# Re-timing a projection, a load and some sums in an attention + FFN kernel whose instructions stay the same

## The chip, the cores and the metric

The kernel runs on one core of a Trainium2 chip. The metric is device time in microseconds (us). TensorE (PE) does the matmuls, VectorE (DVE) and ScalarE (ACT) read their results from PSUM, GpSimd (POOL) issues the loads that also convert f32 to bf16, and SyncE (SP) issues the other DMAs.

## The reference

Linformer attention (8 batches, 8 heads, 1024 tokens, head size 64, keys and values projected to 64 rows), then a feed-forward layer with a squared relu (512 to 2048 to 512):

```python
k_proj = einsum('ks,bhsd->bhkd', E, k);  v_proj = einsum('ks,bhsd->bhkd', F, v)
attn   = softmax(q @ k_proj^T / sqrt(64))          # per batch and head
x      = (attn @ v_proj) as (8*1024, 512)
out    = square(max(x @ w_in, 0)) @ w_out
```

## The kernel before

After a start-up stretch of about 109 us, a steady loop runs on PE: every *step* issues four 128x256 matmuls of the first FFN product (line 652) and, in most steps, four of the second (line 572). Both products use a seven-product (Strassen-like) scheme, so PSUM results are copied from bank to bank, and sums of inputs are formed on DVE. A batch takes 56 steps. Attention for the coming batches is put in between by a plan of steps; PE's order is exactly the order of the code, while the other engines' orders are chosen by a scheduler from the dependencies.

The parts that matter:

```python
def project(self):                       # k and v of a batch, into one PSUM bank
    ps = att_psum()[:, 0]                # (in the loop there is one such buffer)
    for i in range(NI):
        ...matmul(ps[LO, :], lhsT=ET, rhs=self.K...)       # k: partitions 0-63
        ...matmul(ps[HI, :], lhsT=FT, rhs=self.V...)       # v: partitions 64-127
    for g in range(2):
        self.keep_k(ps[LO, ...], g)      # casts "kp", two on DVE for each g
    self.keep_v(ps[HI, :])

def keep_v(self, ps_v):
    nc.scalar.copy(self.vp[HI], view)    # cast "vp" on ACT
    nc.vector.tensor_copy(self.vp[LO], view)

# second FFN product, "second_spread": the seed
yield from product(1, first, True)
nc.scalar.copy(chain, first)             # the seed copy, on ACT
yield
yield
yield from product(2, first, two=True)   # 8 matmuls in a row, may start only after the seed copy
...
# first FFN product, one group = 7 steps: p1, p5, p4 (of the group before), p6, p2, p3, p7
# p1 -> ACT copy; p5, p6 -> ACT copy "u"; p2, p4 -> ACT relu "h"; p3, p7 -> DVE relu-sum "h"
...
for b in range(1, B - 1):                # the plan, t = first step of the batch
    ...
    on(t + 3, b + 1, "sums_spread", 2)   # ends in 8 small DMAs, the "spread copies" rs<-inv
    on(t + 7, b + 1, "values", 0); ... on(t + 23, b + 1, "values", 3)      # DVE needs rs
    for c in range(2):
        at(t + 24 + 9 * c, ... chunk[b + 1, c].sum_x())    # four sums on DVE
    ...
        on(t + 3, b + 3, "load_q")
    on(t + 30, b + 2, "project")
    on(t + 32, b + 2, "transpose_k_dma") # kT<-kp, a transposing DMA, needed at t + 44
        on(t + 34, b + 3, "load_kv")
    on(t + 44, b + 2, "scores", 0)
```

A load goes out when its buffer is free, not at its step: the step sets only its place in POOL's queue.

The softmax here doesn't subtract the row's maximum and nothing guards it: scores larger than these inputs give would overflow.

Of the kernel before, what the change touches and what calls it, by code (L numbers as in the profile page):

```python
# [12 lines left out]
AF = mybir.ActivationFunctionType  # L13
# [6 lines left out]
def kernel(  # L20
# [11 lines left out]
    nc = tc.nc  # L32
# [15 lines left out]
    SCALE = 1.0 / float(D) ** 0.5  # L48
# [26 lines left out]
    def att_psum():  # L75
        turn["att"] += 1
        return pair_psum(turn["att"] % turn["pairs"])

    def bank(shape=(P, 512), dtype=F32, n=None):
        if n is None:  # L80
            turn["bank"] += 1
            n = turn["bank"]
        return psum.tile(list(shape), dtype, tag=f"bank{n % 4}", name="ps_bank")

    def tokens(src, b, h=slice(None), i=slice(None)):
        return src[b].rearrange("h (p i) d -> p h i d", i=NI)[:, h, i, :]

    def load(t, src):
        return nc.gpsimd.dma_start(t, src)

    def load_batch(name, src, b):
        t = qkv_pool.tile([P, H, NI, D], BF16, name=name)
        load(t[:], tokens(src, b))
        return t


# [30 lines left out]
    for j, (lo, hi) in enumerate(W_IN_PIECES):  # L127
        t = wpool.tile([P, NCB, (hi - lo) * P], BF16, name=f"w_in_{lo}")
# [6 lines left out]
    for j in range(WP):  # L135
        if j == WP - 1:
            load(Q0[:, :, 4:8, :], tokens(q, 0, i=slice(4, 8)))
        t = wpool.tile([P, fn, DM], BF16, name=f"w_out_{j}")
# [83 lines left out]
    class Attention:  # L222
# [10 lines left out]
            self.qT = qt_pool.tile([P, H, NT, P], BF16, name="qT")  # L233
            self.e, self.rs, self.ps_x = {}, {}, {}

        def load_kv(self):
            self.K, self.V = load_batch("K_sb", k, self.b), load_batch("V_sb", v, self.b)

        def load_q(self):
            self.Q = load_batch("Q_sb", q, self.b)  # L240


        def keep_k(self, ps_k, g, second=None):
# [96 lines left out]

        def exponentials(self, ps):
            e = soft_pool.tile([P, 2, TCH], BF16, name="expT", tag="expT", bufs=4)
            nc.scalar.activation(e[:], ps[:], AF.Exp, scale=SCALE)  # L343
            return e

        def inverse(self, ps):
# [49 lines left out]
        def values(self, pr, spare=False):  # L396

            e, rs = self.e.pop(pr), self.rs.pop(pr)
            if spare:
                ps_x = [bank(), bank()]  # L400
            else:
                ps = att_psum()
                ps_x = [ps[:, par] for par in range(2)]
            for o, par, a, r in VALUE_QUADS:
                nc.tensor.matmul(  # L405
                    ps_x[par][o], lhsT=self.vp[r, 2 * pr + a, :], rhs=e[r, par], start=True, stop=True
                )
            for par in range(2):
                nc.vector.tensor_tensor(  # L409
                    out=self.xT[:, pr, :, par], in0=ps_x[par].rearrange("p (c t) -> p c t", c=2),  # L410
                    in1=rs[:, par].rearrange("p (c t) -> p c t", c=2), op=ALU.mult,
                )
# [295 lines left out]
    with tc.manual_schedule(engines={PE}):  # L708
# [30 lines left out]
        def at(step, fn, *args, **kwargs):  # L739
            plan.setdefault(step, []).append(lambda: fn(*args, **kwargs))  # L740
# [13 lines left out]
        atts = {0: att}  # L754
        chunk = {(0, c): Chunk(att, c) for c in range(2)}
# [104 lines left out]
        def on(step, b, name, *args):  # L860
            at(step, lambda: getattr(atts[b], name)(*args))

        for b in range(1, B - 1):
            t = 56 * (b - 1)
            if b > 1:
                on(t + 1, b + 1, "scores", 3)
            on(t + 3, b + 1, "sums_spread", 2)
            on(t + 7, b + 1, "values", 0)
            on(t + 10, b + 1, "values", 1)
            on(t + 20, b + 1, "values", 2)  # L870
            on(t + 23, b + 1, "values", 3)
            for c in range(2):
                at(t + 24 + 9 * c, lambda b=b, c=c: chunk[b + 1, c].sum_x())
            if b + 2 < B:
                on(t + 2, b + 2, "transpose_q_dma")
                if b + 3 < B:
                    at(t + 2, begin, b + 3)
                    on(t + 3, b + 3, "load_q")
                on(t + 30, b + 2, "project")
                on(t + 32, b + 2, "transpose_k_dma")  # L880
                if b + 3 < B:
                    on(t + 34, b + 3, "load_kv")
                on(t + 44, b + 2, "scores", 0)
                on(t + 47, b + 2, "scores", 1)
                on(t + 50, b + 2, "sums_spread", 0)
                on(t + 53, b + 2, "scores", 2)
# [34 lines left out]
```

## Time and profile before

482.11 us, median of 3 runs (481.99 to 482.15). From the page: the span, PE's busy time, and the chain of work that ended last by engine.

```profile
span 479.9 us, 10022 instructions
PE 469.9 (98%) x4106; PEld 352.0 (73%) x4106; DVE 350.1 (73%) x613; ACT 286.8 (60%) x466; POOL 32.5 (7%) x45
PE 86%; DVE 8%; ACT 4%; issue 1%; DMA 1%; DVEq 0%; ACTq 0%
```

PE is the limit. How much is still to be had is not told by "98% busy": a pipelined matmul is drawn longer than the time it takes its turn. The Trainium skill ("Trainium Kernel Development and Optimization", Best Practices) says to judge by MFU (the share of the peak matmul rate that is used) and by the busy share of the weight loads, 73% here, and not by that of the matmuls. For small stalls I used another measure, the distance from one start to the next: a 128x256 matmul starts 0.109 us after the one before it, so four take 0.437 us. What exceeds that is a stall, or the change to a differently tiled matmul.

The list of waits, PE alone (columns: us in total, times, longest us):

```profile
PE ps_second L572 <- ACT ps_second L588: 1.3, 5, 0.3
```

The same stall in the timelines, once per batch. PE (start, duration, and in brackets the idle time and what ended it):

```profile
196.59 0.60 PE L572 MATMUL ps_second<-w_out,h 128*128 128x256 bf16 x4
197.03 0.60 PE L652 MATMUL ps_bank<-xT,w_in_sum 128*128 128x256 bf16 x4
197.47 0.60 PE L652 MATMUL ps_bank<-x_sum,w_in_sum 128*128 128x256 bf16 x4
198.33 1.03 PE L572 MATMUL ps_second<-w_out,h 128*128 128x256 bf16 x8 [0.26 <-ACT ps_second L588]
```

The first three groups start 0.44 us apart; product 2 starts 0.86 us after the group before it, so 0.42 us is lost. The bracket says 0.26 because it counts from the drawn end of the matmul. And ACT in the same place:

```profile
195.04 0.60 ACT L662 ACTIVATE h<-ps_bank 128x512 bf16<-128x512 f32 x1 [2.08 <-PE ps_bank L652]
195.97 0.59 ACT L544 COPY u<-ps_bank 128x512 f32<-128x512 f32 x1 [0.33 <-PE ps_bank L652]
196.58 0.58 ACT L251 CAST vp<-ps_att 64x512 bf16<-64x512 f32 x1
197.19 0.60 ACT L662 ACTIVATE h<-ps_bank 128x512 bf16<-128x512 f32 x1
197.69 0.59 ACT L588 COPY ps_second<-ps_second 128x512 f32<-128x512 f32 x1
```

Before a seed that has no projection near it, ACT's timeline has no vp:

```profile
417.10 0.59 ACT L544 COPY u<-ps_bank 128x512 f32<-128x512 f32 x1 [0.33 <-PE ps_bank L652]
417.92 0.60 ACT L662 ACTIVATE h<-ps_bank 128x512 bf16<-128x512 f32 x1 [0.23 <-PE ps_bank L652]
418.41 0.59 ACT L588 COPY ps_second<-ps_second 128x512 f32<-128x512 f32 x1
```

There relu and copy wait for PE, not PE for them. The cast in front of the relu is what makes the seed late.

### The profile page before, as it was taken

To read this page: it belongs to the slowest core of one execution; us is meant where nothing else is said; L and a number is where in the kernel's file an instruction comes from. 1 tells how busy PE (TensorE), PEld (TensorE's weight loads), DVE (VectorE), ACT (ScalarE), POOL (GpSimd) and SP (SyncE) were. 2 spreads that over 40 slices of the span, in tenths; PEclk is the share of its full clock that TensorE was granted. 3 is DMA by queue.
4 is the path that set the end of the run, shared out by engine and by line. 5 is a ranking of instruction groups with operands and counts; after the bars stand their busy time and mean duration, and the time that the engine had idled before them with its cause. 6 is when DMAs were issued, how large, how long until landed. Compare 5 with 4: busy or idle time off the path is not lost.

```text
span 479.9 us, 10022 instructions
## 1 busy us (share of the span) xinstructions
PE 469.9 (98%) x4106; PEld 352.0 (73%) x4106; DVE 350.1 (73%) x613; ACT 286.8 (60%) x466; POOL 32.5 (7%) x45
## 2 busy tenths in 40 slices
PE   8999999999999999999999999999999999999996
PEld 3444445537878788787878778787887778888885
DVE  2456897956996679767897579966797678967671
ACT  2464467397547774578546785477745775565641
POOL 7410010200010000100010000100000000000000
PEclk9999999999999999999999999999999999999999
DMA  9999998999949496767939499495811054101012
GB/s 177 204 206 205 229 165 142 180 225 190 197 83 171 124 200 163 124 130 180 201 105 185 90 221 175 96 160 139 205 54 55 23 133 111 67 23 67 24 66 89
DMA packets 80046, 66.98 MB, mean 140 GB/s; under 512 B 30720, under 2 KB 76032, under 8 KB 80000
## 3 DMA queue, kind: packets, MB, share of 16 engines
q0 software_dynamic: 30640, 29.23, 39.3%
q1 hardware_dynamic: 49216, 36.97, 29.2%
q8 instruction: 32, 0.52, 0.4%
q10 hardware_dynamic: 144, 0.13, 0.1%
q14 instruction: 14, 0.11, 0.1%
HBM read 59.24 MB, written 16.78 MB: 158 GB/s over the span
## 4 chain that ended last, share of the span: by engine, by line
PE 86%; DVE 8%; ACT 4%; issue 1%; DMA 1%; DVEq 0%; ACTq 0%
PE ps_bank L652 34%; PE ps_second L572 33%; PE ps_bank L489 6%; PE ps_att L329 2%; PE ps_att L258 2%; PE ps_second L549 2%; PE ps_att L405 2%; DVE rs L373 1%; DVE w_in_sum L150 1%; DVE w_out_sum L150 1%; DVE xT L434 1%; DVE h L150 1%; PE ps_bank L216 1%; ACT h L485 1%; PE ps_att L382 1%
## 5 line engine op out<-in xcount | busy, mean ns | idle before, releaser
L150 DVE TENSOR_TENSOR h<-h 128x1024 bf16<-128x1024 bf16 (+1 forms) x182 | 108.0, 616 | 39.8 <-ACT h L662 26.0
L652 PE MATMUL ps_bank<-x_sum,w_in_sum 128*128 128x256 bf16 x624 | 93.9, 273 | 0.0
L652 PEld LDWEIGHTS <-w_in_sum 128*128 128x128 bf16 x832 | 78.7, 98 | 16.2 <-issue 7.5
L572 PEld LDWEIGHTS <-h 128*128 128x128 bf16 x832 | 81.3, 98 | 11.8 <-issue 2.2
L544 ACT COPY u<-ps_bank 128x512 f32<-128x512 f32 x107 | 63.2, 591 | 26.0 <-PE ps_bank L652 23.1
L662 ACT ACTIVATE h<-ps_bank 128x512 bf16<-128x512 f32 x104 | 62.9, 605 | 26.3 <-PE ps_bank L652 25.9
L666 DVE CUSTOM_DVE_ANT_0 h<-ps_bank,u 128x512 bf16<-128x512 f32 x104 | 68.9, 685 | 12.5 <-PE ps_bank L652 11.9
L677 ACT COPY ps_bank<-ps_bank 128x512 f32<-128x512 f32 x52 | 29.7, 570 | 68.9 <-PE ps_bank L652 68.9
L652 PEld LDWEIGHTS <-w_in 128*128 128x128 bf16 x624 | 58.8, 98 | 13.9 <-issue 7.2
L572 PEld LDWEIGHTS <-s 128*128 128x128 bf16 x624 | 61.1, 98 | 7.1
L652 PE MATMUL ps_bank<-xT,w_in 128*128 128x256 bf16 x416 | 62.5, 273 | 0.0
L572 PE MATMUL ps_second<-w_out_sum,s 128*128 128x256 bf16 x416 | 62.4, 273 | 0.0
L572 PE MATMUL ps_second<-w_out_sum,h 128*128 128x256 bf16 x416 | 62.2, 273 | 0.0
L572 PE MATMUL ps_second<-w_out,h 128*128 128x256 bf16 x416 | 60.1, 272 | 1.3 <-ACT ps_second L588 1.3
L409 DVE TENSOR_TENSOR xT<-ps_att,rs 128x512 bf16<-128x512 f32 x56 | 36.0, 684 | 15.9 <-PE ps_att L405 15.9
L489 PE MATMUL ps_bank<-xT,w_in 128*128 128x512 bf16 x192 | 45.3, 379 | 1.8 <-DVE xT L434 1.0
L485 ACT ACTIVATE h<-ps_bank 128x512 bf16<-128x512 f32 x48 | 28.1, 605 | 16.1 <-PE ps_bank L489 15.9
L150 DVE TENSOR_TENSOR o_sb<-ps_second,u 128x512 f32<-128x512 f32 x27 | 18.5, 685 | 25.9 <-PE ps_second L572 20.7
L489 PEld LDWEIGHTS <-w_in 128*128 128x128 bf16 x192 | 17.7, 98 | 24.6 <-issue 6.2
L343 ACT ACTIVATE expT<-ps_att 128x1024 bf16<-128x1024 f32 x32 | 32.9, 1036 | 2.9 <-PE ps_att L329 2.5
L652 PE MATMUL ps_bank<-x_sum,w_in 128*128 128x256 bf16 x208 | 31.4, 273 | 0.0
L652 PE MATMUL ps_bank<-xT,w_in_sum 128*128 128x256 bf16 x208 | 31.3, 273 | 0.0
(104 smaller groups left out, 477.7 us busy)
## 6 DMA issues: line engine op xcount, KB each, us to landing
out_dram<-o_sb SPq DMA_DIRECT2D x63, 256.0 KB, 2.4
rs<-inv SPq DMA_DIRECT2D x96, 128.0 KB, 2.9
K_sb<-in_k_dram POOLq DMA_DIRECT2D x7, 1024.0 KB, 9.7
V_sb<-in_v_dram POOLq DMA_DIRECT2D x7, 1024.0 KB, 15.7
Q_sb<-in_q_dram POOLq DMA_DIRECT2D x7, 1024.0 KB, 12.7
w_out<-in_moe_w_out_dram POOLq DMA_DIRECT2D x4, 512.0 KB, 17.5
w_in<-in_moe_w_in_dram POOLq DMA_DIRECT2D x3, 512.0 KB, 14.6
k_f<-in_k_dram SPq DMA_DIRECT2D x1, 512.0 KB, 4.6
```

Source lines behind the costliest of these rows:

```text
L150: return nc.vector.tensor_tensor(out=o, in0=x, in1=y, op=op)
L258: nc.tensor.matmul(ps[LO, :], lhsT=ET[:, i, :], rhs=self.K[:, :, i, :], start=f, stop=l)
L343: nc.scalar.activation(e[:], ps[:], AF.Exp, scale=SCALE)
L409: nc.vector.tensor_tensor(out=self.xT[:, pr, :, par], in0=ps_x[par].rearrange("p (c t) -> p c t", c=2), in1=rs[:, par].rearrange("p (c t) ...
L485: nc.scalar.activation(h, ps.rearrange("p (a t) -> p a t", a=2), AF.Relu)
L489: nc.tensor.matmul(ps[:], lhsT=w_in_blk(cb, fb), rhs=self.xT[:, cb, self.c].rearrange("p a t -> p (a t)"), start=(cb == 0), stop=(cb == NC ...
L544: nc.scalar.copy(u[:], ps)
L572: nc.tensor.matmul(ps[:, i * HM:(i + 1) * HM], lhsT=self.h_form(n, fb)[:, i * P:(i + 1) * P], rhs=w_out_form(n, fb), start=fresh and i == ...
L652: nc.tensor.matmul(ps[:, j * HC:(j + 1) * HC], lhsT=w_in_form(n, cb, 2 * self.g + j), rhs=self.chunk.x_form(n, cb), start=fresh and j == 0 ...
L662: nc.scalar.activation(self.out(kh, a), ps[:], AF.Relu)
L666: nc.vector._custom_dve(TENSOR_ADD_SAT, out=self.out(kh, a), in0=ps[:], in1=more[:], s0=3.0e38, s1=0.0)
L677: nc.scalar.copy(self.chain[:], self.first[:])
```

## The change

Its intent: project k and v two steps sooner, so that the casts are out of the way when the seed is due; hold q's load back from the spread copies; form the second chunk's x sums later, so that DVE is free at the seed.

```diff
-    def load_batch(name, src, b):
+    def load_batch(name, src, b, behind=None):
         t = qkv_pool.tile([P, H, NI, D], BF16, name=name)
-        load(t[:], tokens(src, b))
+        dma = load(t[:], tokens(src, b))
+        if behind:
+            tc.add_manual_dep(dma.ins, behind().ins.name, ..., reason="load behind")
         return t
...
-                nc.vector.tensor_tensor(
+                self.done = nc.vector.tensor_tensor(          # in values()
...
-                at(t + 24 + 9 * c, lambda b=b, c=c: chunk[b + 1, c].sum_x())
+                at(t + 24 + 12 * c, lambda b=b, c=c: chunk[b + 1, c].sum_x())
...
-                    on(t + 3, b + 3, "load_q")
-                on(t + 30, b + 2, "project")
-                on(t + 32, b + 2, "transpose_k_dma")
+                    on(t + 11, b + 3, "load_q", lambda b=b: atts[b + 1].done)
+                on(t + 28, b + 2, "project")
+                on(t + 30, b + 2, "transpose_k_dma")
                 if b + 3 < B:
-                    on(t + 34, b + 3, "load_kv")
+                    on(t + 32, b + 3, "load_kv")
```

No instruction is added or removed. At step t + 11 the last `done` is that of the second pair of heads (`values` at t + 10).

## The prediction

> **What bounds the kernel.** TensorE: the page gives PE busy 469.9 of 479.9 us, and the chain of waits is 86% PE. The Trainium skill ("Trainium Kernel Development and Optimization", Best Practices) says matmul busy time is no measure of headroom; weight loads are busy 73% here. So I read the distance between matmul starts. In the timeline of the steady loop (109 to 411 us, period 55.77 us) the 128x256 products start every 0.109 us. Besides about 0.4 us for each switch to attention's smaller tiles, one stall stands out: five times product 2 of the second stream (8 matmuls, L572) waits for ACT's seed copy (L588). At 198.33 it starts 0.42 us later than the cadence wants; the other four lose as much. Total: 2.1 us. (The list of waits shows 1.3 us, since it counts from the end of the pipelined matmul.)
>
> **Why the seed is late.** ACT's timeline: u at 195.97, v's cast vp (L251, 0.58 us) at 196.58, relu at 197.19, seed at 197.69 to 198.28. Where no projection is near (169.07, 418.41) the order is u, relu, seed; the seed starts 0.37 us after product 1's last matmul starts, against 0.77 us at 197.69, and product 2 loses only 0.01 to 0.03 us. So the cast costs 0.40 us.
>
> **What the change does.** No instruction is added or removed; order moves.
> 1. Projection about 1.75 us earlier. The built order on ACT becomes relu(p4), vp, u(p6), relu(p2), seed: vp goes where ACT idles (2.08 us before 195.04). Estimate from the durations: vp 195.55, u 196.1, relu 196.8, seed 197.3. Worth 5 x 0.40 = 2.0 us, all on PE's path.
> 2. Second chunk's x sums later: two of the four sums (0.42 us each on DVE) come after the relu-sums of p3 and p7 instead of before. Before, p3's relu-sum ends at 199.88 and PE needs the bank at 200.07; with PE 0.4 us earlier this would have become the next wait. Estimate for the new order: it ends near 199.2, needed at 199.65. Earns nothing alone, protects the gain.
> 3. q's load behind DVE's values: it already waited for q's transposing DMA (issued at 174.55); now 1 to 2 us later, used some 45 us later. Worth 0. k and v's loads start 1.75 us earlier. The transposing DMA of k takes 9 us beside them (196.07 to 205.07; 2.3 us at 363.35, where no load runs), needed at 207.15: slack 2 us, should stay over 1.
>
> The first 138 us and the tail keep their order.
>
> **Prediction.** 482.1 - 2.0 = 480.1 us, 0.4% faster; range 479.6 to 481.3. Chances: faster by over 2% 0.01, within 2% 0.97, slower 0.02.
>
> **What would show it.** PE L572's wait for the seed falls from 1.3 us to nearly nothing; the period falls to about 55.37; the seed starts 0.37 us after product 1's last matmul everywhere; matmul counts stay. Step 1 is wrong if the wait stays, step 2 if PE waits for DVE's relu-sum (L666 before) at p5, step 3 if scores wait for kT or DVE's values for rs.
>
> **What would make it wrong.** ACT's and DVE's casts of the projection holding each other up, so that ACT is late again (gain 0 to 1 us); the projection waiting for the attention bank's last values; kT late; DVE's backlog at 186 to 200 us, busy almost without a gap, moving a relu-sum onto PE's path.

## The result, and the profile after

481.11 us, median of 4 runs (479.92 to 481.53), against 482.05 us before. The ratio is 0.998, 95% interval 0.9959 to 1.0002. By time alone this is "the same"; the trace is finer. Line numbers are 5 higher than before. From the page:

```profile
span 479.1 us, 10022 instructions
PE 469.1 (98%) x4096; PEld 351.9 (73%) x4106; DVE 349.2 (73%) x613; ACT 286.2 (60%) x466; POOL 33.3 (7%) x45
PE 86%; DVE 8%; ACT 3%; issue 1%; DMA 1%; DVEq 0%; ACTq 0%
```

(Ten matmul records are missing from this trace; the weight loads, 4106, are all there.) The wait of PE for the seed copy is gone from the list of waits, but not from the cadence. PE's timeline:

```profile
196.73 0.60 PE L577 MATMUL ps_second<-w_out,h 128*128 128x256 bf16 x4
197.16 0.60 PE L657 MATMUL ps_bank<-xT,w_in_sum 128*128 128x256 bf16 x4
197.60 0.60 PE L657 MATMUL ps_bank<-x_sum,w_in_sum 128*128 128x256 bf16 x4
198.22 1.03 PE L577 MATMUL ps_second<-w_out,h 128*128 128x256 bf16 x8
```

Product 2 starts 0.62 us after the group before it, so 0.18 us is still lost where it was 0.42. The period of the loop (seed to seed, 141.91 to 197.69 before and 142.03 to 197.56 after) went from 55.77 to 55.53 us: 0.24 us in each of five batches, 1.2 us in all, not 2.0. The span shows 0.8 because this run's start-up happened to be 0.37 us longer (first seed at 113.67 instead of 113.30): from the first seed to the end of the span it is 366.6 us before and 365.4 after, which is the 1.2. ACT tells why 0.18 us stayed:

```profile
195.18 0.60 ACT L667 ACTIVATE h<-ps_bank 128x512 bf16<-128x512 f32 x1
195.98 0.58 ACT L256 CAST vp<-ps_att 64x512 bf16<-64x512 f32 x1 [0.21 <-DVE kp L252]
196.59 0.58 ACT L549 COPY u<-ps_bank 128x512 f32<-128x512 f32 x1
197.07 0.60 ACT L667 ACTIVATE h<-ps_bank 128x512 bf16<-128x512 f32 x1
197.56 0.61 ACT L593 COPY ps_second<-ps_second 128x512 f32<-128x512 f32 x1
```

The cast vp did move in front of u, as foretold, but ACT then stood idle until DVE's last cast of kp (L252) had ended. DVE's timeline:

```profile
192.64 0.69 DVE L155 TENSOR_TENSOR s<-h 128x1024 bf16<-128x1024 bf16 x1
193.25 0.41 DVE L251 CAST kp<-ps_att 64x256 bf16<-64x256 f32 x1
193.58 0.67 DVE L155 TENSOR_TENSOR s<-s,h 128x1024 bf16<-128x1024 bf16 x1
194.18 0.67 DVE L155 TENSOR_TENSOR h<-h 128x1024 bf16<-128x1024 bf16 x1
194.78 0.41 DVE L252 CAST kp<-ps_att 64x256 bf16<-64x256 f32 x1
195.20 0.42 DVE L251 CAST kp<-ps_att 64x256 bf16<-64x256 f32 x1
195.54 0.41 DVE L252 CAST kp<-ps_att 64x256 bf16<-64x256 f32 x1
```

The projection was done on PE near 192.8, but the scheduler put a sum (`s<-s,h`) and a squaring (`h<-h`), 0.67 us each, between the casts of kp, so the last of them ends at 195.95, and vp at 195.98 follows it at once. In the built program that cast waits on DVE's semaphore alone, not on PE's: two engines' reads of one PSUM bank (the only tile that the two casts share) are put in order. The Trainium skill ("PSUM — Partial Sum Buffer", PSUM bank collisions raise a hardware error) says that reads by ScalarE and VectorE of the same bank and the same 32-partition quadrant collide and that software has to keep them apart, while different quadrants run clean. Here kp is read from partitions 0 to 63 and vp from 64 to 127. No run here tried the two reads at once.

### The profile page after: what moved, and what is told of

Read it like the earlier page. It is cut to its first block, busy times and chain, and to the rows that moved or that the text cites. A ratio compares the mean times of both kernels' runs of the same rounds, so it can differ in the third digit from the quotient of the medians.

```text
span 479.1 us, 10022 instructions
## 1 busy us (share of the span) xinstructions
PE 469.1 (98%) x4096; PEld 351.9 (73%) x4106; DVE 349.2 (73%) x613; ACT 286.2 (60%) x466; POOL 33.3 (7%) x45
## 4 chain that ended last, share of the span: by engine, by line
PE 86%; DVE 8%; ACT 3%; issue 1%; DMA 1%; DVEq 0%; ACTq 0%
PE ps_bank L657 35%; PE ps_second L577 33%; PE ps_bank L494 6%; PE ps_att L334 2%; PE ps_att L263 2%; PE ps_second L554 2%; PE ps_att L410 2%; DVE rs L378 1%; DVE w_in_sum L155 1%; DVE w_out_sum L155 1%; DVE xT L439 1%; DVE h L155 1%; PE ps_bank L221 1%; DMA e_f<-in_E_dram 1%; ACT h L490 1%
```

## The experiments

My theory after the result, A: the wait of ACT's vp for DVE's kp is what left the 0.18 us. Rival B: ACT's u and relu are late on their own. A second question was which part of the change earned the 0.24 us. "Period" is always seed to seed in the trace, a figure that repeated within 0.01 us in undisturbed batches; whole times of one kernel on one chip scatter by 2 to 3 us.

### 1. v's casts first

```diff
-            for g in range(2):
-                self.keep_k(ps[LO, g * C // 2:(g + 1) * C // 2], g)
-            self.keep_v(ps[HI, :])
+            self.keep_v(ps[HI, :])
+            for g in range(2):
+                self.keep_k(ps[LO, g * C // 2:(g + 1) * C // 2], g)
```

> The changed kernel with one more edit: in the projection, v's casts stand before k's casts, so ACT's cast of vp no longer waits for DVE's last cast of kp. Theory A (the 0.18 us that product 2 still loses per batch comes from that wait): ACT's vp starts about 192.8 us, in its idle time; the seed starts 0.37 us after product 1's last matmul; product 2 loses under 0.05 us; the period falls from 55.53 to about 55.37, total gain against the kernel before about 2.0 us. Rival B (seed late because ACT's u and relu are late on their own): vp moves, but product 2 still loses 0.18 us and the period stays 55.53. A side effect to watch under both: DVE casts kp later, so k's transposing DMA starts about 0.5 us later, and its slack ahead of the scores (0.8 to 1.1 us now) falls to 0 to 0.5 us; if it is used up, scores wait for kT.

Measured: period 55.37 in all batches, product 2 loses 0.03 us, the seed starts 0.37 us after product 1's last matmul. A holds, B falls. The slack of k's transposing DMA stayed at 0.7 to 0.8 us, although it was issued later; see experiment 2. The whole time, however, was 480.85 us (before on that chip 481.01; ratio 0.9981, interval 0.9963 to 0.9999), hardly better than the change itself. The list of waits for PE shows what was given back, a wait in the start-up, which uses the same function:

```profile
PE ps_bank L293 <- DVE kp L252: 1.1, 1, 1.1
```

There PE waits for kp at once, and v's cast now delays kp: 1.1 us instead of 0.2.

### 2. ... and the loads of k and v behind k's transposing DMA

To experiment 1 this adds

```diff
-            nc.sync.dma_start_transpose(                       # transpose_k_dma
+            self.done = nc.sync.dma_start_transpose(
-                    on(t + 32, b + 3, "load_kv")
+                    on(t + 32, b + 3, "load_kv", lambda b=b: atts[b + 2].done)
```

> As vfirst, and the loads of the next k and v wait until k's transposing DMA has landed, so that the two do not run at once. If k's transposing DMA takes 9 to 10 us only because the loads run beside it: it lands in 2 to 3 us, slack ahead of the scores over 7 us; period 55.37 or lower if vfirst shows scores waiting for kT, else the same as vfirst. Rival (the transposing DMA is slow by itself when ACT and DVE are busy): still 9 to 10 us to landing.

Measured: period 55.37; 480.16 us, ratio 0.9972 (0.9955 to 0.9990). The view of the tile kT gives the time from issue to landing, first for the changed kernel, then for this one:

```profile
DMA to landing us min/median/max: 2.3/10.1/10.3
```

```profile
DMA to landing us min/median/max: 2.3/2.3/2.4
```

So the 10 us are the company of the loads. The Trainium skill ("DMA: Bandwidth & Descriptors", Issuing engines are not separate DMA queues) says that DMAs of all issuing engines share 16 DMA engines and interleave; these traces agree and give the price for a small transfer beside a large load, a factor of about 4. The slack ahead of the scores went from 0.7 to 7.6 us, which bought no time: it had not been negative.

### 3. v's casts first in the kernel before, projection unmoved

> The kernel before, with only the order of the casts turned (v's before k's); the projection stays where it was. Theory A says that the position of vp's cast on ACT is all that matters for the seed: vp moves ahead of relu(p4), about 194.6 to 195.2, the seed is on time (0.37 us after product 1's last matmul) without moving the projection. But DVE then casts kp 1.3 us later and squares h after that (about 197.3 to 198.0), which product 2 needs at 197.9: I expect a loss of 0 to 0.3 us per batch there, and k's transposing DMA about 1.3 us later, its slack 2.0 falls to about 0.3. Period 55.4 to 55.7. Rival (moving the projection is what matters, not the cast's place): period stays 55.77.

Measured: the seed was on time (0.37 us, loss 0.03), so for the seed the cast's place is what matters, and not the projection's. But the kernel was slower: 484.17 us, ratio 1.0049 (1.0030 to 1.0068), period 56.10, well over the 55.7 that I had allowed. PE's timeline shows two new losses, one inside product 2 (1.16 us where 1.03 is normal) and one at p5, where the bracket says 0.39 us and the distance of starts 0.55:

```profile
199.39 1.16 PE L572 MATMUL ps_second<-w_out,h 128*128 128x256 bf16 x8
201.82 0.60 PE L652 MATMUL ps_bank<-x_sum,w_in_sum 128*128 128x256 bf16 x4 [0.39 <-DVE h L666]
```

I had expected the first and overlooked the second: the casts of kp, now late, push p3's relu-sum (L666), whose bank p5 needs. The projection's earlier place serves DVE, not ACT; experiment 7 shows that moving the sums relieves DVE too.

### 4. The projection's move alone

> The kernel before with the projection (and with it k's transposing DMA and the loads of k and v) two steps earlier, and nothing else of the change. My theory: all of the gain is here, period 55.53, as with the whole change; p3's relu-sum on DVE ends near 199.5, PE needs the bank near 199.9, so no wait yet. Rival (the x sums are needed at this speed already): PE waits for DVE's relu-sum at p5 and the period is above 55.6.

Measured: period 55.53, product 2 loses 0.18 us; 480.14 us, ratio 0.9973 (0.9953 to 0.9993). All of the change's gain per batch is in this part. (Its lower time is a luckier start: first seed at 112.24; from there to the end it is 365.4 us, as with the whole change.)

### 5. The sums' move alone, and the load of q alone

Each is one line (or, for q, the load and its dependency) of the diff applied to the kernel before; one run each.

> The kernel before with the second chunk's x sums twelve steps on and nothing else. Theory: worth nothing alone, since product 2's wait for the seed (0.42 us) leaves the order on ACT as it was: period 55.77. Rival (DVE's backlog delays the casts and through them the seed): the sums' move frees DVE and the loss falls below 0.4 us.

> The kernel before with only the load of q behind the values. Theory: period 55.77, q's load starts 0 to 3 us later in each batch, nobody waits for it. Rival (the load of q slows the spread copies or the transposing DMA, so that moving it pays): period below 55.7, or the spread copies landing sooner.

Measured: period 55.77 in both, product 2 loses 0.42 to 0.43 us in both. Alone, neither is worth anything. Single times, 482.32 and 481.91 us beside 482.77, are within the scatter.

### 6. v's casts first in the loop only

```diff
-        def project(self):
+        def project(self, v_first=False):
...
+            if v_first:
+                self.keep_v(ps[HI, :])
             for g in range(2):
                 self.keep_k(ps[LO, g * C // 2:(g + 1) * C // 2], g)
-            self.keep_v(ps[HI, :])
+            if not v_first:
+                self.keep_v(ps[HI, :])
...
-                on(t + 28, b + 2, "project")
+                on(t + 28, b + 2, "project", True)
```

> The changed kernel with v's casts first, but only for the projections inside the steady loop; before the loop the casts keep their old order. In vfirst the loop took 55.37 us per batch, but the stretch before the loop lost about 1.0 us: there, transposes of kp on PE waited 1.11 us for DVE's cast instead of 0.21 us. Theory: both are had now, period 55.37 and that wait back at 0.21 us; the fixed part before the loop as in the kernel before within its run-to-run scatter; about 2.0 us under the kernel before and about 0.8 us under the changed kernel. Rival (the loss before the loop is part of the scatter of the start): no better than vfirst.

> vfirst_loop again, unedited, beside vfirst_loop_dma on one chip. Expected: period 55.37 in most batches, a ratio to the kernel before of about 0.9955 as at first (0.9952, interval 0.9930 to 0.9973); the difference to vfirst_loop_dma under 0.3 us if the late spread copies are as rare as they look.

> The changed kernel again, unedited, beside the others on one chip, since its first timing had an interval of plus or minus 0.2%. If its gain is 5 times 0.24 us per batch as its trace says, the ratio of the means is near 0.9975, and any further difference is scatter of the start (the first seed copy fell between 112.2 and 114.4 us in six profiled runs whose code there is nearly the same). If the period is not 55.53 again, the reading of the trace was wrong.

Measured, first call, one chip: this version 480.14 us, ratio 0.9952 (0.9930 to 0.9973); the changed kernel again 481.28 us, ratio 0.9981 (0.9961 to 1.0000); the kernel before 482.05 us. In the second, this version gave 480.23 against 481.77 us, ratio 0.9967 (0.9950 to 0.9984). The wait in the start-up is back at 0.2 us, the period, from the second seed on, is 55.37 in all but one batch. Its ACT timeline shows that ACT's idle time before vp is now ended by PE and not by DVE, and PE's that product 2 starts 0.46 us after the group before it:

```profile
192.31 0.58 ACT L256 CAST vp<-ps_att 64x512 bf16<-64x512 f32 x1 [3.46 <-PE ps_att L264]
195.50 0.59 ACT L552 COPY u<-ps_bank 128x512 f32<-128x512 f32 x1 [0.33 <-PE ps_bank L660]
196.31 0.60 ACT L670 ACTIVATE h<-ps_bank 128x512 bf16<-128x512 f32 x1 [0.23 <-PE ps_bank L660]
196.81 0.59 ACT L596 COPY ps_second<-ps_second 128x512 f32<-128x512 f32 x1
```

```profile
196.99 0.60 PE L660 MATMUL ps_bank<-x_sum,w_in_sum 128*128 128x256 bf16 x4
197.45 1.03 PE L580 MATMUL ps_second<-w_out,h 128*128 128x256 bf16 x8
```

By the period this version beats both kernels: five batches times 0.40 us against the kernel before, which is the sum that I had predicted for the change. In the trace of the second the whole of it arrives: 364.6 us from the first seed to the end against 366.6 before. In that of the first it is 365.2, since besides the one late batch PE lost 0.42 us at 114.8, waiting for ACT's inv (L394), which had waited for spread copies. By time it beats the kernel before in both. Its lead over the changed kernel in the first, 1.3 us between the means of six runs each, is barely clear of the scatter (plus or minus 1.3, worked out from the twelve times).

### 7. The sums put back, once the seed is on time; and the sums moved in experiment 3

> vfirst_loop with the second chunk's x sums back at their old step. It tests what the prediction said of them: that they earn nothing alone but become the next wait once PE is 0.4 us earlier. In vfirst p3's relu-sum on DVE ends at 199.96 and PE needs its bank at 200.29; the old step puts one more sum (0.34 us from start to start) ahead of it, so it ends near 200.30. Expected: PE waits at p5 for DVE's relu-sum, 0.05 to 0.15 us per batch, period 55.42 to 55.52. Rival (the sums never mattered): period 55.37.

> The kernel before with v's casts first in the loop and the x sums twelve steps on, the projection unmoved. In vfirst_before (without the sums moved) the seed was on time but PE waited 0.39 us at p5 for DVE's relu-sum of p3, and product 2 came 0.13 us later in its middle: period 56.10. Here the relu-sum stands ahead of three sums and should end near 0.6 us before PE needs it: the wait at p5 goes, only the loss in product 2 (h squared after the casts of kp) stays. Period 55.45 to 55.6. Rival (DVE is late for other work than the sums): the wait at p5 stays above 0.2 us.

Measured: 55.50 in both. In the first, 0.13 us per batch is lost, all of it ahead of p5 and the p4 after it (0.065 us each), because p3's relu-sum comes one x sum later on DVE, and p7's two. In the second, PE no longer waits at p5 (0.39 us by the bracket before), and only product 2's 0.12 us is left. So the sums' move is worth 0.13 us per batch at the pace of experiment 6, 0.6 us in experiment 3 (56.10 to 55.50), and nothing at the pace of the kernel before.

### 8. A late batch in two traces

In the repeat of the changed kernel one batch of four took 56.17 instead of 55.53 us, and in the first trace of experiment 6 one took 55.47. Both times DVE had waited near 242 us for spread copies. The repeat, first DVE, then ACT ten us later:

```profile
242.57 1.29 DVE L414 TENSOR_TENSOR xT<-ps_att,rs 128x512 bf16<-128x512 f32 x2 [1.22 <-DMA rs<-inv]
```

```profile
251.97 0.58 ACT L256 CAST vp<-ps_att 64x512 bf16<-64x512 f32 x1 [0.86 <-DVE kp L252]
```

DVE, which is busy there almost without a gap, carried the 1.2 us along, kp came late, vp waited 0.86 us for it, and product 2 came late. In experiment 6, where vp does not wait for kp, a wait of 0.94 us cost only 0.10 us. Why were the copies late? (The longest that any of the traces shows after the start-up took 9.7 us.) The next version moves the load of q to step t + 24, behind the values of the *last* pair, and has the loads of k and v wait as in experiment 2.

```diff
-                    on(t + 11, b + 3, "load_q", lambda b=b: atts[b + 1].done)
+                    on(t + 24, b + 3, "load_q", lambda b=b: atts[b + 1].done)
```

> vfirst_loop with two loads moved: q's load waits for the values of the last pair instead of the second pair (so all spread copies of the inverse sums have landed), and the loads of k and v wait until k's transposing DMA has landed. Question: why did DVE wait 1.22 us and 0.94 us once each (in the traces of after_again and vfirst_loop, near 242 us) for the last spread copies? Theory: q's load still starts while the last copies are in flight[...]; landing is within 1 us of the need in every batch with a load. Expected: the last copy of each group lands within 3 us of its issue, 5 us or more before it is needed; k's transposing DMA lands in 2 to 6 us; no wait of DVE for rs; period 55.37 in all batches; time as vfirst_loop or up to 0.3 us less. Rival (the copies are slow by themselves behind the stores on the same queue): still 10 us or more.

Measured: the view of the tile rs between 109 and 300 us, where batches have a load of q, first experiment 6, then this one:

```profile
DMA to landing us min/median/max: 2.2/2.6/9.4
```

```profile
DMA to landing us min/median/max: 2.2/2.5/4.1
```

Each group's last copy now lands 2.3 to 2.4 us after its issue and more than 5 us before the values that need it; in all the other kernels it landed 0.1 to 1.8 us before them wherever a load of q was under way. Experiment 2 held back the loads of k and v alone, and its copies still took up to 8.2 us; so it is the load of q, and the rival, the stores on the same queue, which are there in both, falls. k's transposing DMA lands in 2.3 to 3.9 us. No wait for rs, and 55.37 or 55.38 in all batches. The time, 479.67 us, ratio 0.9958 (0.9938 to 0.9978), cannot be told from that of experiment 6 on the same chip (480.23 us, 0.9967): this is insurance, not speed.

### Summary

| version | period, us | product 2 loses, us | ratio to before |
|---|---|---|---|
| before | 55.77 | 0.42 | 1 |
| the change | 55.53 | 0.18 | 0.9980, again 0.9981 |
| its projection alone | 55.53 | 0.18 | 0.9973 |
| its sums alone; its load of q alone | 55.77 | 0.42 | one run each |
| change, v's casts first everywhere | 55.37 | 0.03 | 0.9981 |
| ... with the loads of k and v held back | 55.37 | 0.03 | 0.9972 |
| before, v's casts first everywhere | 56.10 | 0.03 | 1.0049 |
| change, v's casts first in the loop | 55.37 | 0.03 | 0.9952, again 0.9967 |
| ... with the loads of q, k and v held back | 55.37 | 0.03 | 0.9958 |
| change, v's casts first in the loop, its sums put back | 55.50 | 0.03 | one run |
| before, v's casts first in the loop, sums moved | 55.50 | 0.03 | one run |

## Why the prediction was right or wrong, point by point

- **The time**: 480.1 was predicted with 479.6 to 481.3; 481.11 was measured. Right, but by the width of the range: the middle was 1 us too low. There is luck in it too: the first seed alone falls anywhere within 2 us from run to run, the range was 1.7 us wide, and one of the four runs (481.53) lay outside it. By time alone the result can't be told from no change; the period tells it.
- **What bounds the kernel, and why the seed is late**: right. The cast vp costs the seed 0.40 us; experiments 1 and 6 got back exactly that by moving this one cast. A slip of wording: the "0.4 us for each switch to attention's smaller tiles" contains the attention matmuls' own time and is not all switching cost.
- **Step 1, "5 x 0.40 = 2.0 us"**: right mechanism, wrong size. The term that failed is "vp 195.55, u 196.1, ... seed 197.3". Measured: vp 195.98, u 196.59, seed 197.56 (this trace runs about 0.13 us later there). I had vp follow relu(p4) at once, and had not seen that the built program lets it wait for DVE's last cast of kp, which stood behind a sum and a squaring of h. The gain was 0.24 us a batch, 1.2 us in all. I named this danger among what would make it wrong ("casts of the projection holding each other up") and still put the full sum in the middle.
- **Step 2, the sums "earn nothing alone, protect the gain"**: right. Alone 0; at the full pace 0.13 us a batch. At the pace that the change really reached they were not yet needed (experiment 4).
- **Step 3, the loads**: worth 0 alone, right. "Slack 2 us, should stay over 1" was wrong in three of four batches with loads: 0.77, 0.79, 1.09 and 0.92 us, because the transposing DMA took 10.1 instead of 9.0 us. It never became a wait. q's load started 2.9, 1.4 and 0.6 us later in the first three batches and 0.5 us earlier in the fourth, not 1 to 2 us later in each; nobody waited for it. What I did not see is that q's load, "behind" only the second pair, still runs over the last spread copies, which landed 0.1 to 1.5 us before the values that need them; once in the repeat's four batches this cost 0.64 us.
- **"The first 138 us keep their order"**: the order, yes; the time no. The first seed fell between 112.2 and 114.4 us in 14 profiled runs; most kernels share that code. The loads are not the main reason: k's first part landed at 5.80 us in experiment 4 and at 5.83 in experiment 3, but PE's first transposes of q began at 8.37 and 9.85. PE's own pace differed. The same eight matmuls, first in experiment 4, then in experiment 3:

```profile
6.92 1.03 PE L267 MATMUL ps_bank<-K_sb,ET 128*64 128x256 bf16 x8
```

```profile
7.82 1.87 PE L267 MATMUL ps_bank<-K_sb,ET 128*64 128x256 bf16 x8
```

They start 0.109 us apart in the one and 0.214 in the other. In three of the 14 traces (experiments 2, 4 and the first of 6) the pace is the quick one, and the first transposes of q begin at 8.4 to 8.6 us; in the other eleven it is the slow one, and they begin at 9.6 to 10.3. Why the pace differs stays open; the granted clock reads 1.00 there in traces of both kinds. The scatter is as large as the gain, and hides it in a few whole times.

## What to carry to other kernels

When PE starts evenly, read small gains from the period of the loop, and put the gap between starts, not the bracketed wait, into the sum. Before you take an instruction's new start from the idle time of its engine, look at which semaphores the built program gives it: an order of two reads in the source can become a wait of one engine for another. And an edit to a shared function should be costed at every place that calls it: casting v first was worth 0.8 us in the loop and cost about 0.9 us in the start-up.

## What the Trainium skill lacked or had wrong

- "PSUM — Partial Sum Buffer" tells of the collision of reads by ScalarE and VectorE, but not what keeping them apart costs in a pipeline, nor that an ordering per bank makes one engine inherit the other's backlog: here the two orders of the casts lay 0.16 us a batch apart (55.53 against 55.37), and with k's first a batch in which DVE was late lost another 0.64 us (0.10 with v's first).
- "DMA: Bandwidth & Descriptors" says that queues interleave on the same engines; no figure tells what that does to a small transfer. Here a transposing DMA of 128x512 bf16 took 2.3 us alone and 9 to 10 us beside 1 MB bf16 loads, and single 128 KB copies 2.2 to 4.1 us in batches without a load of q and up to 9.7 us beside one.
- "Trainium Kernel Development and Optimization" recommends MFU and the weight loads' share as the measures of distance to the roofline; for stalls of this size the second, the one that I read, is too coarse. It was 73% both before and after, while the period moved by 0.4%. The distance of starts (0.109 us for 128x256) showed each stall.
